# An attention-then-gMLP kernel: transposes moved beside the output product, all masks on VectorE, the first batch re-ordered, unread products in TensorE's queue

## The chip, the cores and the metric

One core of a Trainium2 chip. The metric is the device time of one execution in microseconds (us), lower is better. "Span" is the time from the first to the last instruction of the profiled execution; in the profiled executions of both kernels the device time is 1.8 us more (289.58 and 280.59 us beside spans of 287.8 and 278.8; the prediction took 1.5). The engines are named as the profile names them: PE is TensorE's matmuls, PEld its weight loads, DVE VectorE, ACT ScalarE, POOL GpSimd, SP SyncE. Each engine executes its own queue in order: an instruction that waits holds all that stand behind it (a wait of 5.3 us below shows it).

## The reference, cut to what matters

Eight batches go through windowed attention (8 heads, 576 positions, 64 per head; heads 0 to 3 with a window of 32, heads 4 to 7 with stride 4), then through a gated MLP. `seq` is 576, `d_ff` 1024.

```python
scores = scale * np.matmul(q, k.transpose(0, 1, 3, 2))
scores = np.where(masks, scores, -1e9)          # plain or strided window
attn = softmax(scores)
x = (attn @ v), heads side by side              # 576 x 512
h = gelu(x @ w_in); u, v = halves of h
v_n = (v - mean(v)) / sqrt(var(v) + 1e-6) * g_ln
v_s = w_sg @ v_n + b_sg                         # over the sequence
out = x + (u * v_s) @ w_out
```

## The kernel before

It is written as small steps. Every engine gets its instructions in the order in which the steps are called. The names of the steps in the order texts, with the tile names that the profile shows:

- `T` transposes q and k of one head pair (group) into the PSUM tiles pq, pk and copies them to qT (ACT) and kT or kI (ACT, then DVE); `S` makes the scores pss, exp on ACT gives PT, then the mask is multiplied on;
- `AV` multiplies by v into poa (then rc and onorm on DVE); `X` transposes onorm into xT; `vd` copies v for the strided heads;
- `zv` is the v half of the input product (pz, gelu to vv, statistics st and mv on DVE, then rs on POOL); `vn` normalises; `zu` is the u half (pu);
- `sgu` is the spatial product (pv; then vs and gat on DVE); `out` the output product (po, copied to osb, stored); `W` transposes the spatial weights (pw to wsgT).

The parts that the argument touches, with cuts marked by `...`:

```python
    ps = ctx.enter_context(tc.tile_pool(name="ps", bufs=4, space=bass.MemoryType.PSUM))

    def psum(name):                       # every product takes one of four buffers
        return ps.tile([128, 2, 512], FP32, tag="ps", name=name)
    ...
    def a_S(b, h):
        ...
        eng = nc.gpsimd if b and h % 4 == 3 else nc.vector
        eng.tensor_tensor(PT[:, 0:S], PT[:, 0:S], masks[:, h // 4], AO.mult)
    ...
    for p in range(B + 1):                # sgu and out belong to batch p - 1
        ...
        run("S:0 sgu:0 S:1 S:2 sgu:1 S:3 S:4 sgu:2 S:5 sgu:3 S:6 S:7 gelu", env, io)
        io = LOADS["v"](1) + [(ld_wout,)] if p == 0 else []
        run("AV:0 vd AV:1 out:0 X:0 AV:2 X:1 out:1 AV:3 X:2 T:0 X:3 out:2", env, io)
        io = LOADS["qk"](p + 2) if p + 2 < B else []
        run("zv:0 T:1 zv:1 vn:0 W:0 T:2 zv:2 vn:1 W:1 zu:0 vn:2 T:3 zu:1 W:2 zu:2 W:3 zu:3 W:4",
            env, io)
```

`W` exists in the first batch only. `io` spreads the issues of loads, which stand in GpSimd's queue, among the steps.

The softmax here doesn't subtract the row's maximum and nothing guards it: scores larger than these inputs give would overflow.

## Time and profile before

| | before |
|---|---|
| time, median | 289.31 us (3 runs, 289.23 to 290.4) |
| PE / DVE / ACT / POOL busy | 82% / 69% / 62% / 48% |
| first pz of the first and second batch | 31.13 and 72.60 us |
| from there, pz to pz of the batches | 31.7, 31.7, 31.7, 31.7, 31.5, 31.03 us |
| from the last batch's first pz to the end | 25.9 us |

The lower rows are read from the timeline: the start of the first pz matmul of each batch. They cut the span into one stretch with the loads, six repeats, and a tail. From the page of the kernel before: busy shares, then PE and granted clock by slice (40 equal slices, tenths), then the chain that ended last by engine.

```profile
PE 234.7 (82%) x2494; PEld 167.4 (58%) x2494; DVE 198.7 (69%) x380; ACT 179.2 (62%) x265; POOL 138.9 (48%) x189
...
PE   0467957898889798888889898879889889888883
...
PEclk9998777999999999999999999999999999999998
...
DVE 31%; PE 30%; ACT 13%; DMA 10%; POOL 8%; issue 6%; POOLq 0%; ACTq 0%; DVEq 0%
```

No engine is the bound: the chain passes from one to the other, and the first quarter of the span has an idle TensorE and a lower clock. One caution on every PEclk row and every clock figure of the windows below: the time before a trace's first clock record (22.7 us here) is counted as full clock, but the matmuls there ran at half of it.

From the timeline of before, one steady batch, the start and length in us first, what the engine waited for in brackets: two gats on DVE with a mask on POOL between, and the first output product on PE.

```profile
151.45 0.46 DVE L364 TENSOR_TENSOR gat<-u,vs 128x576 f16<-128x576 f16 x1
...
153.01 1.28 POOL L250 TENSOR_TENSOR PT<-PT,masks 128x576 f16<-128x576 f16 x1 [0.68 <-ACT PT L247]
...
153.41 1.19 DVE L364 TENSOR_TENSOR gat<-u,vs 128x576 f16<-128x576 f16 x1
...
157.34 0.81 PE L374 MATMUL po<-w_out,gat 128*128 128x512 f16 x3 [0.37 <-DVE vs L361]
```

The same gat takes 0.46 us alone and 1.19 us beside a mask on GpSimd. The Trainium skill ("SBUF — State Buffer", section "SBUF: two separate sides") describes a port pair that VectorE and GpSimd share as an exclusive lock; these lines agree with it: the stretched gat ended at 154.60 us, 0.3 us after the mask.

### The profile page before, as it was taken

What the parts mean: (1) busy time and instruction counts of PE and PEld (TensorE: products, weight loads), DVE (VectorE), ACT (ScalarE), POOL (GpSimd) and SP (SyncE); (2) the same over time, 40 slices, a digit from 0 to 9 for tenths busy, and PEclk for the clock granted to TensorE, in tenths of its full rate; (3) what the DMA queues carried; (4) which work ended last, traced back from release to release, by engine and by line L of the source; (5) the groups of instructions that cost most, each with busy time, mean ns of one, the idle gap of its engine ahead of it and who ended that gap; (6) DMA issues with size and microseconds to landing.
All of it is one profiled execution on the core that took longest, in us unless ns stands there. A gap on an engine that the chain in (4) does not pass through costs nothing.

```text
span 287.8 us, 6135 instructions
## 1 busy us (share of the span) xinstructions
PE 234.7 (82%) x2494; PEld 167.4 (58%) x2494; DVE 198.7 (69%) x380; ACT 179.2 (62%) x265; POOL 138.9 (48%) x189
## 2 busy tenths in 40 slices
PE   0467957898889798888889898879889889888883
PEld 0366634766468466666567656756566647754652
DVE  7548347795579839794679748993879557973760
ACT  1366643656786478756787478665876678745502
POOL 8953828481188606890198407970396013200400
PEclk9998777999999999999999999999999999999998
DMA  9999999998169921997079923995099310012004
GB/s 129 133 190 150 155 183 108 103 107 151 53 43 126 184 99 8 95 159 171 18 48 156 156 93 25 108 147 155 16 69 164 122 57 2 2 73 93 0 0 164
DMA packets 91467, 28.92 MB, mean 100 GB/s; under 512 B 71664, under 2 KB 86064, under 8 KB 91440
## 3 DMA queue, kind: packets, MB, share of 16 engines
q0 software_dynamic: 85232, 18.48, 72.3%
q1 hardware_dynamic: 6208, 10.06, 10.3%
q8 instruction: 19, 0.31, 0.4%
q14 instruction: 8, 0.07, 0.1%
HBM read 37.54 MB, written 9.44 MB: 163 GB/s over the span
## 4 chain that ended last, share of the span: by engine, by line
DVE 31%; PE 30%; ACT 13%; DMA 10%; POOL 8%; issue 6%; POOLq 0%; ACTq 0%; DVEq 0%
PE po L374 8%; PE pu L344 8%; DVE vs L361 7%; PE pz L315 7%; DVE gat L364 5%; DVE st L324 5%; DMA w_in<-in_moe_w_in_dram 4%; DVE PT L250 4%; DMA wsg<-in_moe_w_sg_dram 4%; DVE onorm L273 3%; ACT vv L319 3%; POOL kp L123 2%; ACT u L347 2%; PE po L377 2%; ACT osb L380 2%
## 5 line engine op out<-in xcount | busy, mean ns | idle before, releaser
L326 POOL TENSOR_SCALAR rs<-mv 128x2 f32<-128x2 f32 (+1 forms) x24 | 7.2, 300 | 96.8 <-DVE mv L325 96.1
L357 PE MATMUL pv<-wsgT,vn 128*128 128x288 f16 x320 | 45.4, 286 | 7.3 <-DVE vn L334 6.3
L247 ACT ACTIVATE PT<-pss 128x576 f16<-128x576 f32 x64 | 38.5, 650 | 16.5 <-PE pss L243 9.9
L374 PE MATMUL po<-w_out,gat 128*128 128x512 f16 x160 | 42.6, 379 | 5.6 <-DVE gat L364 3.0
L324 DVE BATCH_NORM_STATS2 st<-vv 128x6 f32<-128x512 f32 x40 | 27.2, 681 | 25.2 <-ACT vv L319 24.8
L315 PE MATMUL pz<-w_in,xT 128*128 128x512 f16 x160 | 39.9, 392 | 5.6 <-DVE kT L224 5.6
L380 ACT COPY osb<-po 128x1024 f32<-128x1024 f32 (+1 forms) x24 | 20.9, 870 | 37.4 <-issue 20.9
L357 PEld LDWEIGHTS <-vn 128*128 128x128 f16 x320 | 29.0, 97 | 16.2 <-DVE vn L334 8.6
L344 PE MATMUL pu<-xT,w_in 128*128 128x288 f16 x256 | 35.7, 294 | 2.6 <-ACT u L347 1.6
L344 PEld LDWEIGHTS <-w_in 128*128 128x128 f16 x256 | 25.7, 100 | 11.6 <-issue 3.7
L334 DVE TENSOR_SCALAR vn<-vv,mv,rs 128x512 f16<-128x512 f32 x40 | 22.1, 584 | 13.8 <-POOL rs L327 13.8
L273 DVE TENSOR_TENSOR onorm<-poa,rc 96x768 f16<-96x768 f32 (+1 forms) x32 | 30.6, 956 | 1.1
L319 ACT ACTIVATE vv<-pz 128x1024 f32<-128x1024 f32 (+1 forms) x24 | 21.1, 882 | 14.0 <-PE pz L315 11.6
L347 ACT ACTIVATE u<-pu 128x576 f16<-128x576 f32 x32 | 20.8, 651 | 13.2 <-PE pu L344 13.1
L123 POOL DMA_DIRECT2D qp<-in_q_dram x32 | 25.1, 786 | 6.8 <-DMA wsg<-in_moe_w_sg_dram 3.7
L215 ACT CAST qT<-pq 128x576 f16<-128x576 f32 x32 | 20.4, 638 | 12.3 <-PE pq L204 6.4
L123 POOL DMA_DIRECT2D kp<-in_k_dram x32 | 23.9, 752 | 7.8 <-DMA w_in<-in_moe_w_in_dram 4.1
L315 PEld LDWEIGHTS <-xT 128*128 128x128 f16 x160 | 15.3, 101 | 20.9 <-issue 7.5
L361 DVE SCALAR_TENSOR_TENSOR vs<-pv,g_col,b_bc 128x576 f16<-128x576 f32 x32 | 25.9, 811 | 1.2 <-PE pv L357 1.0
L250 POOL TENSOR_TENSOR PT<-PT,masks 128x576 f16<-128x576 f16 x14 | 17.8, 1273 | 18.2 <-ACT PT L247 18.2
L374 PEld LDWEIGHTS <-gat 128*128 128x128 f16 x160 | 14.4, 100 | 18.9 <-DVE gat L364 7.2
L250 DVE TENSOR_TENSOR PT<-PT,masks 128x576 f16<-128x576 f16 x50 | 21.9, 452 | 4.1 <-ACT PT L247 3.3
(65 smaller groups left out, 442.1 us busy)
## 6 DMA issues: line engine op xcount, KB each, us to landing
out_dram<-osb SPq DMA_DIRECT2D x32, 256.0 KB, 2.3
qp<-in_q_dram POOLq DMA_DIRECT2D x32, 72.0 KB, 3.9
kp<-in_k_dram POOLq DMA_DIRECT2D x32, 72.0 KB, 3.4
qd<-in_q_dram POOLq DMA_DIRECT2D x8, 288.0 KB, 5.5
kd<-in_k_dram POOLq DMA_DIRECT2D x8, 288.0 KB, 6.5
vp<-in_v_dram POOLq DMA_DIRECT2D x8, 288.0 KB, 8.4
vm<-in_v_dram POOLq DMA_DIRECT2D x8, 256.0 KB, 6.5
vt<-in_v_dram POOLq DMA_DIRECT2D x16, 96.0 KB, 6.1
```

What stands on the lines that cost most here:

```text
L123: nc.gpsimd.dma_start(dst, src)
L247: nc.scalar.activation(PT[:, 0:S].rearrange("p (j w) -> p j w", j=2), pss[:, :, 0:HS], AF.Exp, scale=0.125)
L250: eng.tensor_tensor(PT[:, 0:S], PT[:, 0:S], masks[:, h // 4], AO.mult)
L273: nc.vector.tensor_tensor(onorm.rearrange("p a h d -> p h a d"), pv[:, :, :, 0:64], rc.unsqueeze(3).broadcast_to([rows, 2, NB, 64]), AO.mult)
L315: nc.tensor.matmul(pz[:, c, :], xT[:, g4, MT[ti]:MT[ti] + 128], w_in16[:, g4, DH:DFF], start=(g4 == 0), stop=(g4 == 3))
L319: nc.scalar.activation(vv[:, 0:n], pz[:, 0:n], AF.Gelu_apprx_tanh)
L324: nc.vector.bn_stats(st[:, c, :], vv[:, c, :])
L344: nc.tensor.matmul(pu[:, j, 0:HS], w_in16[:, g4, 128 * ph:128 * ph + 128], xT[:, g4, HS * j:HS * j + HS], start=(g4 == 0), stop=(g4 == 3))
L357: nc.tensor.matmul(pv[:, j, 0:HS], vn[:, kp, 128 * ph:128 * ph + 128], wsgT16[:, kp, HS * j:HS * j + HS], start=(kp == 0), stop=(kp == 4))
L361: nc.vector.scalar_tensor_tensor(vs.rearrange("p (j w) -> p j w", j=2), pv[:, :, 0:HS], g_col[:, ph:ph + 1], b_bc.rearrange("p (j w) -> p ...
L374: nc.tensor.matmul(po[:, c, :], gat[:, ph, ts], w_out16[:, ph, :], start=(ph == 0), stop=False)
L380: nc.scalar.copy(osb[:, 0:n], po[:, 0:n])
```

## The change

Its intent, part by part: masks 3 and 7 of each batch after the first go from GpSimd to VectorE; the transposes of the next batch stand beside the output product, so the dense products pz and pu run without interruption; the statistics become a step of their own (`st`) ahead of `vn`; the first batch is re-ordered after the order in which its loads land, the input weights come in two halves, and products of zeros that nobody reads (`w:n`, n of them) stand in TensorE's queue where it would be idle, to keep its clock up. Buffers that were spare are dropped (PT 10 to 8, kT 3 to 2, xT 4 to 2), and some memsets are smaller.

```diff
-        eng = nc.gpsimd if b and h % 4 == 3 else nc.vector
-        eng.tensor_tensor(PT[:, 0:S], PT[:, 0:S], masks[:, h // 4], AO.mult)
+        nc.vector.tensor_tensor(PT[:, 0:S], PT[:, 0:S], masks[:, h // 4], AO.mult)
...
     def ld_win():
-        dma(w_in16, moe_w_in.rearrange("(g p) f -> p g f", p=128))
+        for half in (slice(DH, DFF), slice(0, DH)):
+            dma(w_in16[:, :, half], moe_w_in[:, half].rearrange("(g p) f -> p g f", p=128))
...
+        norm[b, i] = (vv, tis)
+
+    def m_st(b, i):
+        vv, tis = norm.pop((b, i))
...
+    def busy(n):
+        pb = psum("pb")
+        for i in range(n):
+            nc.tensor.matmul(pb[:, 0, :], zeros[:, 0:128], zeros, start=True, stop=True)
...
-    for f, *a in LOADS["qk"](0) + LOADS["v"](0):
+    for f, *a in [(ld_dil, 0), (ld_vd, 0), (ld_plain, 0, 0), (ld_plain, 0, 2),
+                  (ld_vp, 0, 0, 4), (ld_win,), (ld_plain, 1, 0), (ld_plain, 1, 2), (ld_dil, 1), (ld_wsg,)]:
         f(*a)
-    ld_win()
-    for g in range(4):
-        a_T(0, g)
...
+            run("""w:11 T0:2 w:4 T0:3 S:4 w:1 S:5 w:2 S:6 S:7 vd T0:0 w:2 AV:2 w:2 T0:1 AV:3 S:0 w:2
+                   X:2 w:2 S:1 X:3 w:1 S:2 w:1 S:3 w:1 AV:0 w:2 AV:1 w:1 gelu X:0 w:2 X:1 w:3
+                   zv:0 st:0 zv:1 st:1 vn:0 zv:2 st:2 vn:1 LV LVd wout zu:0 vn:2 zu:1 T:0 zu:2
+                   T:1 zu:3 T:2 w:1 T:3 w:2 W:0 W:1 W:2 W:3 W:4 LP:0 LP:2 LD""", env)
+            continue
+        run("S:0 S:1 sgu:0 S:2 S:3 sgu:1 S:4 S:5 sgu:2 S:6 sgu:3 S:7 gelu", env)
+        run("""vd AV:0 LV AV:1 LVd T:0 out:0 LD X:0 AV:2 X:1 T:1 LP:0 out:1 AV:3 X:2 T:2 LP:2 X:3 T:3
+               out:2""", env)
+        run("zv:0 st:0 zv:1 st:1 vn:0 zv:2 st:2 vn:1 zu:0 vn:2 zu:1 zu:2 zu:3", env)
```

`LV`, `LVd`, `LP`, `LD` issue loads of later batches; in the first batch's text `T0` is the first batch's own transposes.

More of the change, by code (lines that the diff above doesn't have):

```diff
@@ L90 @@
     warm = const.tile([128, 1], FP32)
-    NKT = 3
+    zeros = const.tile([128, 512], FP16)
+    NKT = 2
     kTs = [[const.tile([128, HALO + S], FP16, name=f"kT{i}_{hd}") for hd in range(2)]
@@ L102 @@
     vds = [const.tile([KB, 4, NB, 66], FP16, name=f"vd{i}") for i in range(NV)]
-    NPT = 10
+    NPT = 8
     PTb = [const.tile([KB, PTW], FP16, name=f"PT{i}") for i in range(NPT)]
     def setup_consts():
+        nc.vector.memset(zeros, 0.0)
         nc.sync.dma_start(ident16, IDT.ap())
         nc.sync.dma_start(masks, MSK.ap())
-        nc.vector.memset(mhalf, -0.5)
         for i in range(NKT):
@@ L112, in setup_consts @@
                 nc.vector.memset(kTs[i][hd], 0.0)
-            nc.vector.memset(kIs[i], 0.0)
-        for t in vps + vds:
-            nc.vector.memset(t[0:HALO], 0.0)
-            nc.vector.memset(t[:, :, :, 64:65], 1.0)
+        for t in kIs:
+            nc.vector.memset(t, 0.0)
+        for i in range(NV):
+            nc.vector.memset(vps[i][0:HALO, 0, 0, 0:D], 0.0)
+            nc.vector.memset(vps[i][:, :, :, D:D + 1], 1.0)
+            nc.vector.memset(vds[i][:, :, :, D:D + 1], 1.0)
         for t in PTb:
             nc.vector.memset(t[:, S:PTW], 1.0)
+        nc.vector.memset(mhalf, -0.5)
         nc.vector.memset(wsgT16[0:64, 4, :], 0.0)
@@ L127, in open_batch @@
     def open_batch(b):
+        if b in loaded:
+            return
         qp = ld.tile([QB, NB, 4, D], FP16, tag="qp", name="qp")
@@ L134, in ld_plain @@
     def ld_plain(b, h0):
-        if h0 == 0:
-            open_batch(b)
+        open_batch(b)
         for t, src in zip(loaded[b][0], (q, k)):
@@ L141, in ld_dil @@
     def ld_dil(b):
+        open_batch(b)
         for t, src in zip(loaded[b][1], (q, k)):
@@ L279, in a_X @@
         onorm = onorms.pop((b, g))
-        if g == 0:
-            xTs[b] = sb.tile([128, 4, S], FP16, tag="xT", name="xT", bufs=4)
+        if b not in xTs:
+            xTs[b] = sb.tile([128, 4, S], FP16, tag="xT", name="xT", bufs=2)
         xT = xTs[b]
@@ L319, in m_zv @@
         nc.scalar.activation(vv[:, 0:n], pz[:, 0:n], AF.Gelu_apprx_tanh)
+        norm[b, i] = (vv, tis)
+    def m_st(b, i):
+        vv, tis = norm.pop((b, i))
+        n = len(tis)
         st = sb.tile([128, 2, 6], FP32, tag="st", name="st", bufs=3)
@@ L383, in m_out, with run @@
             nc.sync.dma_start(out[b][MT[ti] + lo:MT[ti] + 128, :], osb[lo:128, c, :])
+    def busy(n):
+        pb = psum("pb")
+        for i in range(n):
+            nc.tensor.matmul(pb[:, 0, :], zeros[:, 0:128], zeros, start=True, stop=True)
     def gelu_table():
         nc.scalar.activation(warm, mhalf[:, 0, :], AF.Gelu_apprx_tanh)
-    LOADS = {"qk": lambda b: [(ld_plain, b, 0), (ld_plain, b, 2), (ld_dil, b)],
-             "v": lambda b: [(ld_vp, b, 0, 4), (ld_vd, b)]}
-    def run(text, env, io):
-        steps = text.split()
-        done = 0
-        for i, step in enumerate(steps):
-            while done < len(io) and done * len(steps) <= i * len(io):
-                f, *a = io[done]
-                f(*a)
-                done += 1
+    def run(text, env):
+        for step in text.split():
             name, _, n = step.partition(":")
@@ L404, in run @@
                 f(*a, *([int(n)] if n else []))
-        for f, *a in io[done:]:
-            f(*a)
     setup_consts()
-    for f, *a in LOADS["qk"](0) + LOADS["v"](0):
+    for f, *a in [(ld_dil, 0), (ld_vd, 0), (ld_plain, 0, 0), (ld_plain, 0, 2),
+                  (ld_vp, 0, 0, 4), (ld_win,), (ld_plain, 1, 0), (ld_plain, 1, 2), (ld_dil, 1), (ld_wsg,)]:
         f(*a)
-    ld_win()
-    for g in range(4):
-        a_T(0, g)
     for p in range(B + 1):
@@ L417 @@
             env |= {"S": (a_S, p), "AV": (a_AV, p), "X": (a_X, p), "vd": (cp_vd, p),
-                    "zv": (m_zv, p), "vn": (m_vn, p), "zu": (m_zu, p)}
+                    "zv": (m_zv, p), "st": (m_st, p), "vn": (m_vn, p), "zu": (m_zu, p)}
         if p + 1 < B:
-            env["T"] = (a_T, p + 1)
-        if p == 0:
-            env["W"] = (prep_wsg,)
+            env |= {"T": (a_T, p + 1), "LV": (ld_vp, p + 1, 0, 4), "LVd": (ld_vd, p + 1)}
+        if p + 2 < B:
+            env |= {"LP": (ld_plain, p + 2), "LD": (ld_dil, p + 2)}
         if p >= 1:
@@ L425 @@
         if p == 0:
-            io = LOADS["qk"](1) + [(ld_wsg,)]
-        else:
-            io = LOADS["v"](p + 1) if p + 1 < B else []
-        run("S:0 sgu:0 S:1 S:2 sgu:1 S:3 S:4 sgu:2 S:5 sgu:3 S:6 S:7 gelu", env, io)
-        io = LOADS["v"](1) + [(ld_wout,)] if p == 0 else []
-        run("AV:0 vd AV:1 out:0 X:0 AV:2 X:1 out:1 AV:3 X:2 T:0 X:3 out:2", env, io)
-        io = LOADS["qk"](p + 2) if p + 2 < B else []
-        run("zv:0 T:1 zv:1 vn:0 W:0 T:2 zv:2 vn:1 W:1 zu:0 vn:2 T:3 zu:1 W:2 zu:2 W:3 zu:3 W:4",
-            env, io)
+            env |= {"T0": (a_T, 0), "W": (prep_wsg,), "w": (busy,), "wout": (ld_wout,)}
+            run("""w:11 T0:2 w:4 T0:3 S:4 w:1 S:5 w:2 S:6 S:7 vd T0:0 w:2 AV:2 w:2 T0:1 AV:3 S:0 w:2
[7 more added lines that the diff above has]
+        run("zv:0 st:0 zv:1 st:1 vn:0 zv:2 st:2 vn:1 zu:0 vn:2 zu:1 zu:2 zu:3", env)
 _INS = ['q', 'k', 'v', 'moe_w_in', 'moe_g_ln', 'moe_w_sg', 'moe_b_sg', 'moe_w_out']
```

## The prediction

> **What bounds it now.** No engine alone: the page has TensorE busy 82%, VectorE 69%, ScalarE 62%, but the chain of waits is 31% VectorE, 30% TensorE, 13% ScalarE, 10% DMA. By the timeline, the second batch's first gMLP product ("pz") starts at 72.8 us; six intervals of 31.7 (four), 31.5 and 31.0 us follow; then 25.7 us. The windows give 27.8 us of TensorE and 23.7 us of VectorE work in each 31.7.
>
> **First batch: gain of about 9 us.** Now "pz" starts at 31.1 after input weights landed at 25.6; then the chain goes through the spatial-weight DMA (10.5 us), and GpSimd starts the first rs at 43.7, though the mean was ready near 36.6, because it stood in blocked DMA issues. The second batch's masks start at 55.5. After: input weights come in two halves, attention goes in order of landing, rs ops precede the later DMA issues. I put the first "pz" near 24 us and the next batch's masks near 41 to 46. Steady work from there puts the second "pz" at about 63.5 instead of 72.8. The granted clock, 0.78 and 0.90 in the windows 20 to 31 and 31 to 73 us, should rise to nearly 1.0; the Trainium skill ("TensorE: Matmul & The Clock Gate", "Part 1: The HAM clock gate") has the clock halved after idle windows. The unread products (0.22 us each warm, about 40) stand mostly in DMA waits.
>
> **Steady batches: slower by about 1 us.** Read from one batch: pz 1.73 per pair, pu 1.0, transposes 0.52 per group, pv 1.23, output 1.09 per tile, masks 0.37 start to start, vs 0.84, gat 0.37.
> - The products without transposes last 8.3 us on TensorE instead of 11.0; masks start 11.0 us after pz, not 13.9.
> - Two masks return to VectorE (+0.74), but two gats stretched to about 1.1 to 1.2 us beside a GpSimd mask fall back to 0.46. The skill ("SBUF — State Buffer") describes an exclusive port pair shared by both engines; the trace agrees. Net −0.6.
> - The vd copies (0.74) now precede the first reciprocal. The first onorm ends near 20.9 us, and the first output product now reuses that accumulator's buffer (four rotate), so TensorE stands about 2.2 us; now it starts at 21.2 without that wait.
> - Three more transpose groups, 1.6 us, lie among the output products. The last output waits about 1 us for T:2's second copy to free its buffer.
> Sum: 8.3 + 12.7 + 9.8 + 2 of stalls = 32.7 against 31.7.
>
> **End.** The seventh interval has no transposes in its second half: about 28.3 to 29 instead of 31.0. Tail unchanged, 25.7.
>
> Total: 63.5 + 5 × 32.7 + 28.5 + 25.7 + 1.5 (time over span) = 282.7; I say **282 us**, range **275 to 288.5**. Chances: faster by over 2% 0.62, within 2% 0.34, slower 0.04.
>
> **Right if:** pz-to-pz intervals of 32 to 33.5 us; TensorE's waits show the first output product waiting for onorm and the last for a key copy on VectorE; no idle inside pz and pu; gat near 0.46 everywhere; clock near 1.0 from about 8 us; first pz before 26 us, second near 63.5.
>
> **Wrong if:** intervals stay at 31.7 or fall (the stalls overlap something I added): then 275 to 277. Or the loads land later than I assume, or the fillers hold ready work: then 286 to 288. Removing buffers (PT 10 to 8, kT 3 to 2, xT 4 to 2) should cost nothing: their readers finish a batch earlier.

## More of the kernel before

From the waits of before between 28 and 56 us, in the first batch (who waited, for whom, us in total, times, longest):

```profile
DVE vn L334 <- POOL rs L327: 5.5, 1, 5.5
...
PE pw L186 <- DMA wsg<-in_moe_w_sg_dram: 2.9, 1, 2.9
```

The first normalisation waited 5.5 us for rs, and TensorE 2.9 us at `W:0` for the spatial weights to land.

## The result, and the profile after

The changed kernel takes 280.31 us (median of 4 fast runs, 280.0 to 281.46) against 289.38 us for the kernel before beside it (4 runs). The ratio is 0.9687, with a 95% interval of 0.965 to 0.9723. Ratios here are the mean time of one kernel's fast runs over that of the other's of the same rounds, so not quite the ratio of the medians.

| us | before | predicted | after |
|---|---|---|---|
| first pz of the first batch | 31.1 | 24 | 30.2 |
| first mask of the second batch | 55.5 | 41 to 46 | 48.9 |
| first pz of the second batch | 72.6 | 63.5 | 69.6 |
| next five intervals together | 158.3 | 163.5 | 155.2 |
| sixth interval | 31.0 | 28.5 | 28.0 |
| tail | 25.9 | 25.7 | 25.9 |
| sum with the prediction's 1.5 | 289.3 | 282.7 | 280.3 |

The total was met within 2 us, but by luck, through two terms that miss in opposite directions: 6.1 us too little for the first stretch, 8.3 us too much for the five intervals. One more caution: moving the transposes shifts work over the boundary pz. Three groups of the third batch's transposes now lie ahead of the second pz, and the sixth interval has lost its own. Cut at the first mask of each batch, the first stretch gained 6.6 us (55.48 to 48.92), the following six intervals together 2.5 us (189.5 to 187.0), and the rest nothing (42.8 to 42.9).

The page of the changed kernel, the lines that answer to those of before:

```profile
PE 240.2 (86%) x2534; PEld 168.1 (60%) x2534; DVE 189.3 (68%) x388; ACT 177.7 (64%) x265; POOL 122.7 (44%) x176
...
PE   6489988978988898979988898979988998989883
...
PEclk9689995999999999999999999999999999999999
...
DVE 33%; PE 25%; ACT 18%; DMA 9%; issue 8%; POOL 5%; POOLq 0%; ACTq 0%; DVEq 0%
```

PE has work from the first slice (the unread products). By the clock records its clock still falls to half twice in the first 50 us, from 8.7 to 15.6 and from 42.9 to 49.7 us. The first eleven unread products were over at 5.8 us, 4 us before the first transpose.

All gats of the changed kernel (the view of one tile: min/median/max in ns), then one steady batch from the timeline, second transpose and first output product:

```profile
L375 DVE TENSOR_TENSOR gat<-u,vs x32: 457/457/459, 51.2 to 268.8; 128x576 f16<-128x576 f16 x32
```

```profile
149.16 0.42 PE L211 MATMUL pq<-ident,qp 96*128 96x96 f16 x6
150.16 0.42 PE L211 MATMUL pk<-ident,kp 96*128 96x96 f16 x6 [0.57 <-DVE vs L372]
151.01 1.02 PE L385 MATMUL po<-w_out,gat 128*128 128x512 f16 x4 [0.44 <-ACT qT L222]
```

No gat is stretched any more, as predicted. The first output product waited 0.44 us for the copy of qT (which stood on ScalarE behind a table load of 1.28 us), not 2.2 us for onorm. All that PE's matmuls waited for between 131.83 and 163.01 us, one interval:

```profile
PE pv L368 <- DVE vn L345: 0.7, 1, 0.7
PE pk L211 <- DVE vs L372: 0.6, 1, 0.6
PE po L385 <- ACT xT L307: 0.5, 1, 0.5
PE poa L272 <- DVE onorm L279: 0.5, 1, 0.5
PE po L385 <- ACT qT L222: 0.4, 1, 0.4
PE pxt L292 <- DVE kT L231: 0.3, 1, 0.3
PE po L385 <- ACT xT L295: 0.2, 1, 0.2
```

### The profile page after: what moved, and what is told of

It reads as the page before. It is cut to its first block, busy times and chain, and to the rows that moved or that the text cites. A ratio compares the mean times of both kernels' runs of the same rounds, so it can differ in the third digit from the quotient of the medians.

```text
span 278.8 us, 6220 instructions
## 1 busy us (share of the span) xinstructions
PE 240.2 (86%) x2534; PEld 168.1 (60%) x2534; DVE 189.3 (68%) x388; ACT 177.7 (64%) x265; POOL 122.7 (44%) x176
## 4 chain that ended last, share of the span: by engine, by line
DVE 33%; PE 25%; ACT 18%; DMA 9%; issue 8%; POOL 5%; POOLq 0%; ACTq 0%; DVEq 0%
PE po L385 8%; DVE st L335 8%; PE pz L321 7%; DVE onorm L279 5%; DVE vs L372 4%; DMA qd<-in_q_dram 4%; DVE PT L256 4%; DMA kd<-in_k_dram 3%; DVE vn L345 3%; ACT osb L391 3%; ACT vv L325 3%; ACT xT L307 2%; PE pv L368 2%; ACT PT L254 2%; DVE gat L375 2%
## 5 line engine op out<-in xcount | busy, mean ns | idle before, releaser
L337 POOL TENSOR_SCALAR rs<-mv 128x2 f32<-128x2 f32 (+1 forms) x24 | 8.6, 358 | 102.3 <-DVE mv L336 102.3
L368 PE MATMUL pv<-wsgT,vn 128*128 128x288 f16 x320 | 46.3, 289 | 5.8 <-DVE vn L345 5.2
L254 ACT ACTIVATE PT<-pss 128x576 f16<-128x576 f32 x64 | 38.4, 652 | 18.5 <-PE pss L250 14.8
L385 PE MATMUL po<-w_out,gat 128*128 128x512 f16 x160 | 41.5, 379 | 9.3 <-ACT qT L222 3.4
L321 PE MATMUL pz<-w_in,xT 128*128 128x512 f16 x160 | 35.9, 379 | 0.0
L256 DVE TENSOR_TENSOR PT<-PT,masks 128x576 f16<-128x576 f16 x64 | 27.7, 453 | 8.3 <-ACT PT L254 7.5
L355 PE MATMUL pu<-xT,w_in 128*128 128x288 f16 x256 | 33.0, 286 | 0.3 <-ACT u L358 0.3
L279 DVE TENSOR_TENSOR onorm<-poa,rc 128x768 f16<-128x768 f32 (+1 forms) x32 | 30.6, 955 | 1.1
L231 DVE CAST kI<-pk 64x576 f16<-64x576 f32 x16 | 12.9, 806 | 24.8 <-ACT kI L230 24.8
L385 PEld LDWEIGHTS <-gat 128*128 128x128 f16 x160 | 14.6, 98 | 21.6 <-issue 9.6
L127 POOL DMA_DIRECT2D qp<-in_q_dram x32 | 24.1, 767 | 5.1 <-DMA vp<-in_v_dram 2.4
L345 DVE TENSOR_SCALAR vn<-vv,mv,rs 128x512 f16<-128x512 f32 x40 | 19.9, 532 | 3.8 <-POOL rs L338 3.8
## 6 DMA issues: line engine op xcount, KB each, us to landing
qd<-in_q_dram POOLq DMA_DIRECT2D x8, 288.0 KB, 7.8
kd<-in_k_dram POOLq DMA_DIRECT2D x8, 288.0 KB, 9.1
vp<-in_v_dram POOLq DMA_DIRECT2D x8, 288.0 KB, 5.6
```

What stands on the lines that cost most here:

```text
L127: nc.gpsimd.dma_start(dst, src)
L254: nc.scalar.activation(PT[:, 0:S].rearrange("p (j w) -> p j w", j=2), pss[:, :, 0:HS], AF.Exp, scale=0.125)
L256: nc.vector.tensor_tensor(PT[:, 0:S], PT[:, 0:S], masks[:, h // 4], AO.mult)
L279: nc.vector.tensor_tensor(onorm.rearrange("p a h d -> p h a d"), pv[:, :, :, 0:64], rc.unsqueeze(3).broadcast_to([rows, 2, NB, 64]), AO.mult)
L321: nc.tensor.matmul(pz[:, c, :], xT[:, g4, MT[ti]:MT[ti] + 128], w_in16[:, g4, DH:DFF], start=(g4 == 0), stop=(g4 == 3))
L355: nc.tensor.matmul(pu[:, j, 0:HS], w_in16[:, g4, 128 * ph:128 * ph + 128], xT[:, g4, HS * j:HS * j + HS], start=(g4 == 0), stop=(g4 == 3))
```

## The experiments

All ran beside the kernel before (medians 289.2 to 289.5 us); the changed kernel was not run again beside them. "First mask" is that of the second batch, "interval" the range of the four pz-to-pz times from the third batch to the seventh. All results are correct. Every profile quoted is fast, except the one of the eighth run, whose figures from the trace are marked with a star.

| run | time, median | ratio to before (95%) | first mask | interval |
|---|---|---|---|---|
| before | 289.38 | 1 | 55.48 | 31.5 to 31.7 |
| after | 280.31 | 0.9687 (0.965 to 0.9723) | 48.92 | 30.9 to 31.2 |
| e1_rotate | 301.44 | 1.0411 (1.0369 to 1.0453) | 52.45 | 34.1 to 34.4 |
| e2_masks_pool | 292.30 | 1.0115 (1.0073 to 1.0158) | 49.14 | 32.0 to 32.2 |
| e3_t_in_c | 282.73 | 0.9758 (0.9711 to 0.9805) | 49.07 | 31.1 |
| e4_old_batch0 | 286.45 | 0.9888 (0.9857 to 0.9919) | 54.81 | 30.9 to 31.2 |
| e5_no_fill | 281.35 | 0.9712 (0.968 to 0.9745) | 48.28 | 30.9 to 31.2 |
| e6_before_masks | 285.24 | 0.985 (0.9817 to 0.9882) | 56.16 | 30.9 to 31.1 |
| e7_late_loads | 284.37 | 0.9821 (0.9793 to 0.9849) | 53.52 | 30.9 to 31.1 |
| e8_new1 | 287.14 | 0.9901 (0.9859 to 0.9942) | 48.74* | 31.9 to 33.8* |
| e9_w_last | 277.09 | 0.9575 (0.9558 to 0.9592) | 46.26 | 30.9 to 31.1 |
| e10_new4 | 279.24 | 0.9653 (0.9621 to 0.9685) | 48.43 | 30.7 |
| e11_new2 | 280.31 | 0.9714 (0.9653 to 0.9774) | 48.06 | 31.2 |
| e12_best | 275.52 | 0.9529 (0.9492 to 0.9566) | 46.05 | 30.7 |

### Where the hand sum of the steady batch failed: buffers in strict turn

The prediction assumed that the four PSUM buffers are taken in turn, so that the first output product gets the one of the first AV and waits for its onorm. The built program shows otherwise: from one steady batch to the next the buffers follow no fixed turn, and the first output product gets the buffer of the pq just before it. In the trace above the copy to qT on ScalarE frees that buffer at 150.96 us, and the product starts at 151.01; the first onorm ends only at 152.90. This run forces the strict turn.

```diff
     def psum(name):
-        return ps.tile([128, 2, 512], FP32, tag="ps", name=name)
+        turn[0] += 1
+        return ps.tile([128, 2, 512], FP32, tag=f"ps{turn[0] % 4}", name=name, bufs=1)
```

> The changed kernel with the four PSUM buffers taken in strict turn, as the prediction assumed. Theory (the prediction's stall was right for a strict turn, only the buffers are not handed out so): the first output product waits for onorm on VectorE, each steady interval from pz to pz rises from 31.1 to 32.3 to 33 us, the time from 280.3 to 287 to 291 us. Rival (which buffer is taken does not matter, the hand sum was wrong elsewhere): intervals stay within 0.3 us of 31.1, time 280 to 281 us.

Measured: 301.4 us, intervals of 34.1 to 34.4 us. PE's waits between 144.33 and 178.76 us:

```profile
PE po L388 <- DVE onorm L282: 2.1, 1, 2.1
PE po L388 <- DVE kI L234: 0.9, 1, 0.9
...
```

Both stalls are the ones that the prediction named, in size too (2.2 and about 1 us). The interval is 34.4 us, 1.7 us longer than the 32.7 of the hand sum. The windows of the same interval tell why (window, its length, busy us of PE, PEld, DVE, ACT, POOL with instructions, then the granted clock):

```profile
162.20:165.62 3.42, 0.93 (x19) 0.69 (x17) 3.35 (x8) 2.24 (x4) 2.36 (x4) 1.00 1.53 175
...
165.62:169.03 3.41, 3.41 (x12) 1.48 (x13) 1.80 (x3) 0.00 (x0) 1.21 (x2) 0.50 2.11 134
```

TensorE was busy for 0.93 of 3.42 us, and for the next 3.41 us the clock was half. The first output product took from 165.62 to 169.47, 3.85 us, against 2.17 us (151.01 to 153.18) in the changed kernel: 1.7 us more, and 34.4 minus 1.7 is 32.7. So the stalls that the hand sum foresaw are real for buffers in strict turn, and the buffers are what it had wrong. That the sums agree to a tenth is partly luck: 1.7 us is a difference between two traces, and the sum counts 2 us of stalls where its own list names 3.2 and the waits show 3.0. The Trainium skill ("TensorE: Matmul & The Clock Gate", section "Part 1: The HAM clock gate") has a clock that halves after a window of about 3.4 us without work; the length agrees with this trace (3.41 us at half clock), but here TensorE was not idle all through the 3.42 us before it. The same page's section "A second HAM failure mode: psum-queue depth-cycling" tells of a clock that oscillates where TensorE idles briefly and often between groups of matmuls; this trace lies between the two, with one wait of 2.1 us and one of 0.36 us in that stretch.

### The masks

```diff
-        nc.vector.tensor_tensor(PT[:, 0:S], PT[:, 0:S], masks[:, h // 4], AO.mult)
+        eng = nc.gpsimd if b and h % 4 == 3 else nc.vector
+        eng.tensor_tensor(PT[:, 0:S], PT[:, 0:S], masks[:, h // 4], AO.mult)
```

> The changed kernel with masks 3 and 7 of each batch after the first back on GpSimd. Theory (two gats are stretched from 0.46 to about 1.1 to 1.2 us again, which costs VectorE more than the two masks saved): steady intervals 31.5 to 31.8 us instead of 31.1, time 283 to 285 us. Rival (VectorE is not what the intervals wait for): intervals 31.0 to 31.2, time 280 to 281 us.

Measured: 292.3 us, 12 us more than the changed kernel and more than the kernel before. Intervals rise by about 0.95 us, more than expected, and the second batch alone costs 5.7 us more (first mask to first mask 37.45 us instead of 31.79). There the masks on GpSimd stand behind load issues. From the timeline of this run, POOL and DVE:

```profile
53.10 0.72 POOL L127 DMA_DIRECT2D kp<-in_k_dram  x1 [2.52 <-DMA w_out<-in_moe_w_out_dram]
...
55.95 2.50 POOL L257 TENSOR_TENSOR PT<-PT,masks 128x576 f16<-128x576 f16 x2
```

```profile
55.02 3.76 DVE L257 TENSOR_TENSOR PT<-PT,masks 128x576 f16<-128x576 f16 x1
```

GpSimd's two masks come late and together, and a VectorE mask beside them lasts 3.76 us instead of 0.45. Over the whole run twelve of the 32 gats are stretched, six of them to 1.37 to 1.54 us, where 1.1 to 1.2 us was expected. The mirror run puts that one part of the change alone into the kernel before:

```diff
-        eng = nc.gpsimd if b and h % 4 == 3 else nc.vector
-        eng.tensor_tensor(PT[:, 0:S], PT[:, 0:S], masks[:, h // 4], AO.mult)
+        nc.vector.tensor_tensor(PT[:, 0:S], PT[:, 0:S], masks[:, h // 4], AO.mult)
```

> The kernel before with one part of the change alone: all masks on VectorE. Theory (the masks are what the steady batches gained from): intervals 31.0 to 31.2 us instead of 31.7, no gat above 0.5 us, time 285 to 287 us. Rival (the masks help only together with the new order): intervals 31.5 to 31.8, time 288.5 to 290 us.

Measured: 285.2 us, intervals 30.9 to 31.1 us. The masks alone give all that the steady batches gained, with every transpose at its old place. They are worth 4 us in the old order and 12 us in the new one. Of these 12 us 5.7 lie in the second batch, where GpSimd's masks stood behind waiting loads, and about 0.95 in each later interval.

### The place of the transposes

```diff
-        run("""vd AV:0 LV AV:1 LVd T:0 out:0 LD X:0 AV:2 X:1 T:1 LP:0 out:1 AV:3 X:2 T:2 LP:2 X:3 T:3
+        run("""vd AV:0 LV AV:1 LVd out:0 LD X:0 AV:2 X:1 LP:0 out:1 AV:3 X:2 T:0 LP:2 X:3
                out:2""", env)
-        run("zv:0 st:0 zv:1 st:1 vn:0 zv:2 st:2 vn:1 zu:0 vn:2 zu:1 zu:2 zu:3", env)
+        run("zv:0 st:0 T:1 zv:1 st:1 vn:0 T:2 zv:2 st:2 vn:1 zu:0 vn:2 T:3 zu:1 zu:2 zu:3", env)
```

> The changed kernel with the transposes of the steady batches back at the places of before (one group beside the output product, three among pz and pu). Theory (the move is near neutral: the transposes cost TensorE about as much in either place): steady intervals 31.0 to 31.5 us, time 280 to 283 us. Rival (the move is what made the steady batches faster): intervals back to 31.7 or more, and the time 284 us or more.

Measured: steady intervals of 31.06 us, no different. In the steady batches the move earns nothing. The median is 2.4 us above the changed kernel's. In the trace the difference lies in the second batch (first mask to first mask 34.36 us instead of 31.79). The waits of this run between 67 and 100 us name it:

```profile
POOL kp L127 <- DMA qd<-in_q_dram: 5.0, 2, 3.2
DVE vn L345 <- POOL rs L338: 3.5, 2, 3.1
```

A load issue in GpSimd's queue waited up to 3.2 us for an earlier load, and the normalisation waited 3.1 us for an rs behind it. This trace is of an execution of 283.6 us; two of the four took 281.1 and 281.8 us, so the loss is not the same in each.

### The first batch

First the old first batch under the new steady order: old loads, one load of the input weights, no unread products, and this order of steps (for a batch without predecessor the `sgu` and `out` steps are empty):

```diff
-            run("""w:11 T0:2 w:4 T0:3 S:4 w:1 S:5 w:2 S:6 S:7 vd T0:0 ...
+            run_io("S:0 S:1 S:2 S:3 S:4 S:5 S:6 S:7 gelu", env, LOADS["qk"](1) + [(ld_wsg,)])
+            run_io("AV:0 vd AV:1 X:0 AV:2 X:1 AV:3 X:2 T:0 X:3", env, LOADS["v"](1) + [(ld_wout,)])
+            run_io("zv:0 st:0 T:1 zv:1 st:1 vn:0 W:0 T:2 zv:2 st:2 vn:1 W:1 zu:0 vn:2 T:3 zu:1 W:2 zu:2 W:3 zu:3 W:4",
+                   env, LOADS["qk"](2))
```

> The changed kernel with the first batch as it was before: old order of loads and steps, input weights in one load, no unread products; all later batches as changed. Theory (most of the gain is in the first batch): the second batch's first mask starts at 54 to 56 us instead of 48.9, time 286 to 288 us. Rival (the first batch only looked faster and the steady order earns the gain): time 282 to 284 us.

Measured: first mask at 54.81 us, 286.45 us. So about 6 us of the change's 9 us lie in the first batch. The next two runs take apart what in it. First only the third batch's loads are moved out from among the normalisations:

```diff
-                   env, LOADS["qk"](2))
+                   env, [])
+            for f, *a in LOADS["qk"](2):
+                f(*a)
```

> The same as the run with the old first batch (286.5 us), with one difference: the third batch's query and key loads are issued after the first batch's last step and no longer among its normalisations. Theory (the first batch lost most because rs stood behind loads in GpSimd's queue): the first rs starts near 36 to 38 us instead of 43.0, the second batch's first mask at 50 to 52 us instead of 54.8, time 281.5 to 284 us. Rival (the order by landing and the unread products earn the gain of the first batch): first mask within 1 us of 54.8, time 285.5 us or more.

The first rs of the old first batch and of this run, from their timelines:

```profile
43.03 0.23 POOL L337 TENSOR_SCALAR rs<-mv 128x2 f32<-128x2 f32 x1
```

```profile
33.85 0.22 POOL L337 TENSOR_SCALAR rs<-mv 128x2 f32<-128x2 f32 x1 [0.30 <-DVE mv L336]
```

Measured: the first rs starts at 33.85 us instead of 43.03, yet the first mask comes only 1.3 us earlier, at 53.52 us; 284.4 us. As a step the theory holds (rs is free), as an explanation it fails: another wait took over. PE's longest wait in this run, between 28 and 56 us:

```profile
PE pw L193 <- DMA wsg<-in_moe_w_sg_dram: 5.3, 1, 5.3
```

`W:0` stood behind the second of the three pz steps, the spatial weights landed only at 38.4 us, and everything behind `W:0` in TensorE's queue waited with it. So the five `W` steps go to the end of the batch, and nothing else changes:

```diff
-            run_io("zv:0 st:0 T:1 zv:1 st:1 vn:0 W:0 T:2 zv:2 st:2 vn:1 W:1 zu:0 vn:2 T:3 zu:1 W:2 zu:2 W:3 zu:3 W:4",
+            run_io("zv:0 st:0 T:1 zv:1 st:1 vn:0 T:2 zv:2 st:2 vn:1 zu:0 vn:2 T:3 zu:1 zu:2 zu:3 W:0 W:1 W:2 W:3 W:4",
```

> The same as the run with the old first batch and late loads (284.4 us), with one more difference: the five transposes of the spatial weights stand behind the first batch's last product, not among its normalisations. Theory (TensorE stood 5.3 us in its own queue for the spatial weights' load, 33.2 to 38.5 us, with ready products behind): no such wait, the second batch's first mask at 48.5 to 50.5 us instead of 53.5, time 279.5 to 281.5 us, so that order of landing and unread products are worth nothing beside it. Rival (the wait only moves: the load lands when it lands, and the order of attention by landing is needed): first mask at 52.5 us or later, time 283 us or more.

Measured: first mask at 46.26 us, 277.09 us, both lower than either theory said and lower than the changed kernel. From this run's timeline, the last product of the first batch and the spatial weights behind it:

```profile
38.30 3.10 PE L355 MATMUL pu<-xT,w_in 128*128 128x288 f16 x24 [0.22 <-ACT u L358]
41.24 0.42 PE L193 MATMUL pw<-ident,wsg 96*128 96x96 f16 x6
```

TensorE does not wait for the load at all. The gain at the first mask, 7.3 us, is more than the wait of 5.3 us. The windows from 33.20 us to the first mask, of the run before and of this one, show a second difference (the granted clock is the number after the five engines):

```profile
33.20:53.52 20.32, 12.61 (x126) 9.30 (x127) 11.61 (x22) 8.95 (x13) 12.57 (x19) 0.83 1.38 129
```

```profile
33.20:46.26 13.06, 10.23 (x119) 7.49 (x118) 12.17 (x24) 10.07 (x15) 8.86 (x14) 1.00 1.72 174
```

With the wait the clock fell as well (half from 37.4 to 44.2 us); without it the clock stayed full. So part of the 7.3 us may be the clock; how large a part was not tested by itself. Two moves in the old first batch, loads behind rs and `W` behind the products, give 8.5 us (54.81 to 46.26). The changed kernel has both moves, together with the order by landing, the two halves and the unread products, and reaches only 48.92 us. From the first pz to that mask it takes 18.7 us, against 16.5 here; in that stretch its clock is half from 42.9 us on, and here it is full. Of what it does more, only the unread products were tried alone (next run, 0.6 us at the first mask); the order by landing and the halves were not. Whether `W` last alone, with rs still behind the loads, would do as much was not run.

The unread products by themselves:

```diff
     def busy(n):
+        return
         pb = psum("pb")
```

> The changed kernel without the unread products. Theory (they stand where TensorE waits, and a warm clock there is worth little, as the chain of the first batch runs over VectorE, ScalarE and the loads): the granted clock of the first 70 us falls to 0.8 to 0.9, the second batch's first mask moves by less than 1 us from 48.9, time 279.5 to 282 us. Rival (the clock is what the first batch gained from): first mask of the second batch 3 us or more later, time 283 us or more.

Measured: 281.35 us, with single runs of 279.7 to 282.4; the interval of its ratio overlaps that of the changed kernel, so no effect on the time is to be seen in either direction. The trace shows two effects that cancel. From the timelines, without and with the unread products, the first batch's pz matmuls:

```profile
27.97 0.38 PE L321 MATMUL pz<-w_in,xT 128*128 128x512 f16 x1
28.87 5.75 PE L321 MATMUL pz<-w_in,xT 128*128 128x512 f16 x19 [0.51 <-ACT xT L295]
```

```profile
30.21 4.52 PE L321 MATMUL pz<-w_in,xT 128*128 128x512 f16 x20
```

Without them pz starts 2.2 us earlier and then runs partly at the low clock; with them it starts later, at full clock. Both end near 34.7 us. The windows of this run grant full clock up to 28.5 us, but its first clock record is at 21.6 us, and before it equal matmuls take longer:

```profile
20.11 0.67 PE L240 MATMUL pss<-qT,kT 128*128 128x96 f16 x6
21.55 0.46 PE L240 MATMUL pss<-qT,kT 128*128 128x96 f16 x6
```

In the first line one matmul takes 281 ns and starts 80 ns after the last; in the second, from 21.64 us on, they take 206 ns and start about 43 ns apart. So without the unread products the clock was half up to 21.6 us, and again for two stretches of 3.4 us. Counted as half from the start, that gives an estimate of 0.80 for the first 70 us: the expected fall did come, and it cost no time that can be seen.

### Attempts at a better kernel

The first attempt pulls the spatial products ahead of the last scores, moves the gelu table load behind the first transposes' copies and the `vd` copies behind the first two onorms, and puts both AV pairs ahead of the second output product.

```diff
-        run("S:0 S:1 sgu:0 S:2 S:3 sgu:1 S:4 S:5 sgu:2 S:6 sgu:3 S:7 gelu", env)
-        run("""vd AV:0 LV AV:1 LVd T:0 out:0 LD X:0 AV:2 X:1 T:1 LP:0 out:1 AV:3 X:2 T:2 LP:2 X:3 T:3
+        run("S:0 S:1 S:2 sgu:0 S:3 sgu:1 S:4 sgu:2 S:5 sgu:3 S:6 S:7", env)
+        run("""AV:0 LV AV:1 LVd T:0 gelu out:0 vd LD X:0 X:1 AV:2 AV:3 T:1 LP:0 out:1 X:2 T:2 LP:2 X:3 T:3
```

> A version meant to beat both: the changed kernel, in the steady batches with the spatial products pulled ahead of the last scores (gat 3 no longer behind eight masks), the gelu table load behind the first transposes' copies, the vd copies behind the first two onorms, and both AV pairs ahead of the second output product. Theory (TensorE waits at the first output product for the copy of qT behind the table load, and for onorm after it): intervals 29.3 to 30.5 us instead of 31.1, time 272 to 277 us. Rival (VectorE's chain to the second onorm is as long as before and holds all that follows): intervals 30.8 to 31.3, time 279 to 281 us.

Measured: a miss, 287.1 us over four runs, one of them slow; the three fast ones took 285.6 to 288.0 us, all slower than the changed kernel. Why the fast runs are slower stays open. The second attempt is one edit: from the second batch on the `vd` copies run on ScalarE, behind the first transposes' copies.

```diff
-        nc.vector.tensor_copy(vd[:, :, 0:4, 0:D], vm)
-        nc.vector.tensor_copy(vd[:, :, 4:6, 0:D], vt[:, :, 0:3:2, :])
+        cp = nc.scalar.copy if b else nc.vector.tensor_copy
+        cp(vd[:, :, 0:4, 0:D], vm)
+        cp(vd[:, :, 4:6, 0:D], vt[:, :, 0:3:2, :])
...
-        run("""vd AV:0 LV AV:1 LVd T:0 out:0 ...
+        run("""AV:0 LV AV:1 LVd T:0 vd out:0 ...
```

> The changed kernel with one edit: from the second batch on the vd copies run on ScalarE behind the first transposes' copies, no longer on VectorE before the first reciprocal. Theory (VectorE's chain from the first mask to the second onorm holds the second half of attention): the chain is 0.74 us shorter, intervals 30.3 to 30.6 us instead of 31.1, time 275 to 277.5 us. Rival (the next wait takes it over): intervals 30.9 to 31.2, time 279.5 to 281 us.

Measured: intervals of 30.74 us, about 0.35 us less, half of what the theory expected. The waits of poa for onorm and of pxt for kT are gone from PE's list (0.5 and 0.3 us). What is left in an interval, for matmuls:

```profile
PE pv L369 <- DVE vn L346: 0.7, 1, 0.7
PE pk L212 <- DVE vs L373: 0.6, 1, 0.6
PE po L386 <- ACT xT L308: 0.5, 1, 0.5
PE po L386 <- ACT qT L223: 0.4, 1, 0.4
```

The third attempt adds to it the edits below, and a copy of the first spatial weight tile on ScalarE.

```diff
-        run("S:0 S:1 sgu:0 S:2 S:3 sgu:1 S:4 S:5 sgu:2 S:6 sgu:3 S:7 gelu", env)
-        run("""AV:0 LV AV:1 LVd T:0 vd out:0 ...
+        run("S:0 S:1 sgu:0 S:2 S:3 sgu:1 S:4 S:5 sgu:2 sgu:3 S:6 S:7", env)
+        run("""AV:0 LV AV:1 LVd T:0 gelu vd out:0 ...
```

> The run before it, with three more edits: the fourth spatial product ahead of the last two scores, the gelu table load behind the first transposes' copies, and one of the five spatial weight copies on ScalarE. Theory: the first output product starts about 0.8 us earlier, but the following onorm does not, so intervals 30.0 to 30.5 us, time 273 to 277 us. Rival (the added idle time of TensorE makes the granted clock fall in some batches, as in the first attempt): intervals above 31, clock below 1.0 in the windows, time 280 us or more.

Measured: intervals of 31.24 us, 0.5 us worse than without these edits, and 280.3 us; a miss. Interval and time are as the rival said, but the granted clock stays at the top tenth from about 49 us on, so the rival's reason does not hold, and what the intervals lost was not taken apart. The last run joins the two that won: `e9_w_last` with the `vd` copies on ScalarE.

> The two winners together: the run with the spatial weights' transposes last (277.1 us, intervals 30.9 to 31.1) and the vd copies on ScalarE (intervals 30.74). If their gains are separate (one in the first batch, one in each of six intervals): intervals 30.7 to 30.8, second batch's first mask near 46.3 us, time 274.5 to 276.0 us. If they get in each other's way: 276.5 us or more.

Measured: 275.52 us (274.6 to 277.6), ratio 0.9529. Intervals of 30.73 to 30.74 us, first mask at 46.05 us. The gains are separate and add up (3.2 and 1.1 us alone, 4.8 together), and this version beats both kernels. It has no unread products and the first batch's loads in the old order.

## Why the prediction was right or wrong

- **No engine alone bounds the kernel.** Held: after the change the chain is still shared (DVE 33%, PE 25%, ACT 18%).
- **First batch, "gain of about 9 us", first pz near 24 us, masks at 41 to 46 us, second pz at 63.5 us.** Right in direction, too large: 30.2, 48.9 and 69.6 us. The term that failed is the time to the first pz: it is 6.2 us off, while from there to the second pz 39.5 us were predicted and 39.4 measured. The first load, now issued first, gave TensorE its first transpose at 9.74 us, against 7.23 us for the smaller load that came first before. The unread products alone hold the first pz back by 2.2 us. And the named causes were not the main one: freeing rs gave 1.3 us when tried alone, while taking `W` out of the middle of TensorE's queue then gave 7.3 us. The prediction saw the spatial weights' load in the chain but not that TensorE stood in its queue for it.
- **The clock "should rise to nearly 1.0" from about 8 us.** Wrong: it was half from 8.7 to 15.6 us, and again from 42.9 to 49.7 us. The unread products at the head of the queue ended at 5.8 us and the first transpose came at 9.74, so in the 3.41 us before the first fall PE worked 0.43 us. From the first to the second pz the windows give 0.91.
- **"Steady batches: slower by about 1 us", 32.7 us.** Wrong: 30.9 to 31.2 us. The step that failed is "the first output product now reuses that accumulator's buffer (four rotate)". The buffers are not handed out in turn. Where they are forced to be, the two predicted stalls stand in the waits with 2.1 and 0.9 us, and the interval, less what the halved clock adds to the output product, is 32.7 us. In their place the changed kernel's first output product waits 0.44 us, for the copy of qT.
- **Masks and gats.** Right in mechanism: every gat takes 0.46 us. Mis-sized: net 0.6 us per batch was predicted, and the masks alone measured 0.6 to 0.8 us per interval in the old order and about 0.95 us in the new.
- **Moving the transposes gains nothing in a steady batch by itself.** The predicted sum for it was a loss; the run with them moved back shows 31.06 us, neither gain nor loss, in an interval. Products without idle time came as predicted: pz waited 0.0 us and pu 0.3 us in all.
- **Sixth interval 28.3 to 29 us, tail unchanged.** Nearly right: 28.0 us, a little below the range, and 25.9 us where 25.7 was said.
- **Fewer buffers cost nothing.** Not tested by a run of its own. ScalarE and VectorE write these buffers; in the changed kernel, between 131.83 and 163.01 us, none of their writes to kT or kI waits for a score, and those to PT wait only for pss and the exp.

Of the seven signs that the prediction lists under "Right if", two came (no idle time inside pz and pu, gats near 0.46 us) and five did not. The total was right by luck: the first stretch was 6.1 us too optimistic and the five intervals 8.3 us too pessimistic. The profile shows this only when the span is cut into stretches; from the total alone the story of the prediction would have looked confirmed.

## What to carry to other kernels

An instruction that waits for a load belongs behind the work that is ready, in every in-order queue: here, with rs freed first, moving five small transposes of late weights behind the first batch's products gave 7.3 us, and the kernel that also re-orders its loads and fills gaps with unread products was slower than the one that does not (280.3 and 277.1 us). Before costing a stall for a reused buffer, look up in the built program which buffer the tile really gets. And check a prediction by its terms, not its total.

## What the Trainium skill lacked or had wrong

- "TensorE: Matmul & The Clock Gate", "Part 1: The HAM clock gate": it names idle windows of about 3.4 us as what halves the clock, and "A second HAM failure mode: psum-queue depth-cycling" many short idle times, without numbers for them. Here the longest single wait was 2.1 us, and a stretch of 3.42 us with 0.93 us of PE work was followed by 3.41 us at a clock of 0.50. In the changed kernel even 2.19 us of PE work in 3.41 us (39.45 to 42.86 us) was followed by half the clock. How much work within a window keeps the clock is not stated.
- "SBUF — State Buffer", "SBUF: two separate sides": it says that the loser of the shared port pair blocks fully. The gats agree (0.46 us to 1.19 us beside one mask on GpSimd), but a VectorE mask of 0.45 us that started 0.93 us before two GpSimd masks (2.50 us together) lasted 3.76 us, longer than both. GpSimd issued loads just before; no run separates their part.
- None of the pages that this case drew on says that tiles of one PSUM pool need not get its buffers in turn. Here strict turn made an interval 3.2 us longer (on average 34.3 instead of 31.1 us, 1.7 us of it in the one trace read being the clock).
